# Sliding-window attention with an MLP-mixer: attention scores on half of the array's rows, the first heads loaded as float32, and new instruction orders

## The chip, the cores and the metric

The kernel runs on one core of a Trainium2 chip. The metric is the device time of one execution in microseconds (us), over several executions; the median is quoted with the lowest and highest.

## The reference, cut to what matters

```python
# B, H, S, D = 8, 8, 576, 64; window 128
scores = q @ k.T / sqrt(D) + slope[h] * -abs(i - j)     # only 0 <= i - j < 128, else -1e9
attn   = softmax(scores) @ v                            # [8, 8, 576, 64]
x  = attn, heads side by side                           # [8, 576, 512]
u  = x + (relu(x.T @ w_tok1) @ w_tok2).T                # token mix   576 -> 256 -> 576
out = u + relu(u @ w_ch1) @ w_ch2                       # channel mix 512 -> 1536 -> 512
```

A block of 128 keys meets only its own 128 queries and the next 128. That makes a 128 x 256 block of scores for each head and key block. 576 is four chunks of 128 and a tail of 64.

## The kernel before: the parts that matter

TensorE contracts over the partitions, the 128 rows of its array. A head has only D = 64 of them. The kernel keeps two heads (a "head pair") on top of each other in one `kT` tile and pads q with zeros, so that one full matmul gives both heads' scores side by side:

```python
psS = [PS(f"psS{i}", [P, 512]) for i in range(2)]      # PSUM: two score banks
psO = PS("psO", [P, 2, 512])                           # PSUM: probabilities times v
qT  = [T(f"qT{i}", [P, NC, NHP, 2, P]) for i in range(2)]   # head 0: rows 0-63, head 1: rows 64-127, rest 0
# ... cut
def score(b, kb, hp):                                  # one key block, one head pair
    # ... cut
    lhsT = kT[i][:, kb, hp, :]                         # 128 rows: head 0 over head 1
    if kb < NC - 1:
        nc.tensor.matmul(s[:, :], lhsT=lhsT, rhs=qT[i][:, kb:kb + 2, hp, :, :],   # 512 columns
                         start=True, stop=True)
    # ... cut: last key block (256 + 128 columns) and tail (128)
    nc.scalar.activation(out=e[:, 0:nn], in_=s[:, 0:nn], func=ACT.Exp, scale=scale)
    # ... cut: DVE multiplies by the mask, one head pair at a time
```

The order of all work of a batch is written out as a list of names. One prime is one batch ahead. `S` are scores, `A` transposes of q and k on TensorE (batches 0 and 1), `Lk Lq Zk Zq` loads of k and q and their DMA transposes (later batches), `v` a chunk of v, `P` probabilities times v, `K U X` the token mix, `C` and `D` the two channel matmuls, `T` and `E` their tails, `H0 H1` the two halves of the second channel weight. A list for the steady state, before:

```python
PERIOD = """
S33' T0 Zk'' C0 C1 C5 C3 P2' C7 v0''' C2 S40' Zq'' C6 P3' C4 C9 S41' C10 Lk''' v4''' C8 S42'
# ... cut
S23'' X0' S30'' E0 E1 E2 D30 D31 S31'' D32 S32''
"""
```

The softmax here doesn't subtract the row's maximum and nothing guards it: scores larger than these inputs give would overflow.

## Time and profile before

| | before |
|---|---|
| device time, median of 4 runs beside the changed kernel | 317.18 us (316.64 to 319.14) |
| profiled span | 314.4 us |
| TensorE (PE) busy, matmuls | 289.1 us, 2469 |
| first channel matmul starts | 40.08 us |
| two steady batches | 68.70 us |

How to read it: the device time is nearly all TensorE, but "busy" hides what a matmul costs. A matmul's record is about 400 ns long for 512 columns, yet the next one starts 215 ns later. So I count starts, not busy time. Two groups of the page show what the change aims at (line, engine, operation, output<-inputs, shapes, count | busy us, mean ns | idle before and what ended it):

```profile
L281 ACT ACTIVATE pe<-psS 128x512 bf16<-128x512 f32 (+2 forms) x160 | 78.2, 514 | 92.6 <-PE psS L271 37.6
L271 PE MATMUL psS<-qT,kT 128*128 128x512 bf16 x96 | 35.9, 400 | 3.4 <-ACT qT L239 1.8
```

There are 96 score matmuls that stream 512 columns each, half of them against zeros, and 160 exponentials.

### The profile page before, as it was taken

Reading aid. Unit: us, or ns where it says so; the run is one execution under the profiler, and the core shown is the slowest. Engines: PE = TensorE matmul, PEld = TensorE weight load, DVE = VectorE, ACT = ScalarE, POOL = GpSimd, SP = SyncE. Lnnn points to the kernel's source line nnn. Section 1 sums busy time; section 2 is a strip of 40 time slices with the busy share of each in tenths; the row PEclk is TensorE's granted clock in tenths of the full one; section 3 lists DMA queues with packets and bytes.
Section 4 is the critical chain, followed back from the end, with each engine's and each line's share of the span. In section 5 each row is a group of like instructions: output and inputs, shape, how many; then the busy total and the mean of one; then the engine's idle time right before and its main releaser. Section 6 shows DMA issues by size and latency. Waiting matters only on the chain.

```text
span 314.4 us, 6324 instructions
## 1 busy us (share of the span) xinstructions
PE 289.1 (92%) x2469; PEld 160.0 (51%) x2490; DVE 196.9 (63%) x478; ACT 130.5 (42%) x269; POOL 125.5 (40%) x166
## 2 busy tenths in 40 slices
PE   1677795999999999999999999999999999999995
PEld 1255543645564555546554555545554555545443
DVE  4468565958874866559674847568756937553521
ACT  4757575506442643346333552345235632212200
POOL 8996796309805950882097304850000000000000
PEclk9999999999999999999999999999999999999999
DMA  7999999989997998999499929991740120001013
GB/s 95 141 198 196 183 159 151 134 201 138 169 181 80 149 171 137 192 160 130 110 190 168 89 69 211 162 162 38 176 85 33 70 67 2 33 35 67 2 67 100
DMA packets 152381, 38.52 MB, mean 122 GB/s; under 512 B 139552, under 2 KB 147872, under 8 KB 152352
## 3 DMA queue, kind: packets, MB, share of 16 engines
q0 software_dynamic: 103664, 17.80, 82.6%
q1 hardware_dynamic: 48688, 20.32, 28.8%
q8 instruction: 19, 0.31, 0.4%
q14 instruction: 10, 0.08, 0.1%
HBM read 35.85 MB, written 9.44 MB: 144 GB/s over the span
## 4 chain that ended last, share of the span: by engine, by line
PE 78%; DMA 10%; POOL 8%; issue 2%; DVE 1%; SPq 0%; POOLq 0%
PE psM L483 25%; PE psM L435 23%; DMA vp<-in_v_dram 7%; PE psS L271 5%; PE psM L378 4%; PE psM L393 3%; PE psM L505 3%; DMA qT<-qn 3%; PE psT L450 3%; PE psO L315 2%; PE psM L425 2%; POOL vp L166 2%; PE psO L311 2%; POOL ks L176 1%; PE psM L380 1%
## 5 line engine op out<-in xcount | busy, mean ns | idle before, releaser
L281 ACT ACTIVATE pe<-psS 128x512 bf16<-128x512 f32 (+2 forms) x160 | 78.2, 514 | 92.6 <-PE psS L271 37.6
L483 PE MATMUL psM<-WC,r 128*128 128x512 bf16 x359 | 89.1, 379 | 0.7
L435 PE MATMUL psM<-utb,WC 128*128 128x512 bf16 x384 | 89.1, 379 | 0.2 <-ACT qT L239 0.2
L438 DVE TENSOR_SCALAR r<-psM 128x512 bf16<-128x512 f32 x72 | 49.6, 690 | 20.0 <-PE psM L435 18.8
L435 PEld LDWEIGHTS <-WC 128*128 128x128 bf16 x384 | 35.5, 98 | 37.4 <-issue 0.2
L483 PEld LDWEIGHTS <-r 128*128 128x128 bf16 x372 | 35.2, 98 | 37.6 <-issue 0.2
L286 DVE TENSOR_TENSOR pb<-pe,masks 128x512 bf16<-128x512 bf16 x96 | 39.4, 419 | 10.7 <-ACT pe L281 10.3
L186 POOL DMA_DIRECT2D qn<-in_q_dram x48 | 35.9, 771 | 23.2 <-DMA qT<-qn 12.8
L166 POOL DMA_DIRECT2D kn<-in_k_dram x24 | 21.1, 905 | 55.6 <-DMA kT<-kn 54.2
L488 DVE TENSOR_TENSOR ob<-psM,ub 128x512 f32<-128x512 f32 x31 | 21.4, 692 | 32.1 <-PE psM L483 31.9
L271 PE MATMUL psS<-qT,kT 128*128 128x512 bf16 x96 | 35.9, 400 | 3.4 <-ACT qT L239 1.8
L166 POOL DMA_DIRECT2D vp<-in_v_dram x32 | 29.1, 937 | 2.1 <-DMA qs<-in_q_dram 0.8
L441 ACT ACTIVATE r<-psM 128x512 bf16<-128x512 f32 x24 | 14.3, 597 | 23.1 <-PE psM L435 23.0
L395 DVE TENSOR_TENSOR ub<-psM,xb 128x512 bf16<-128x512 f32 x28 | 18.7, 684 | 2.7 <-PE psM L393 2.7
L325 DVE TENSOR_TENSOR xb<-psO,rt 128x512 bf16<-128x512 f32 x28 | 19.4, 692 | 1.0
L315 PE MATMUL psO<-vp,pb 128*128 128x65 bf16 x224 | 15.9, 193 | 3.5 <-DMA vp<-in_v_dram 3.5
L315 PEld LDWEIGHTS <-pb 128*128 128x128 bf16 x224 | 13.4, 97 | 6.8 <-issue 4.4
L393 PE MATMUL psM<-r,W 128*128 128x512 bf16 x50 | 14.4, 379 | 0.1
L378 PE MATMUL psM<-xb,W 128*128 128x512 bf16 x56 | 14.4, 379 | 0.0
L271 PEld LDWEIGHTS <-kT 128*128 128x128 bf16 x96 | 9.3, 99 | 9.8 <-issue 3.2
L450 PE MATMUL psT<-utt,WC 128*128 128x64 bf16 x384 | 13.8, 193 | 0.0
L450 PEld LDWEIGHTS <-WC 128*128 128x128 bf16 x384 | 12.9, 98 | 1.6 <-issue 0.2
(121 smaller groups left out, 338.7 us busy)
## 6 DMA issues: line engine op xcount, KB each, us to landing
out_dram<-ob SPq DMA_DIRECT2D x31, 256.0 KB, 2.2
vp<-in_v_dram POOLq DMA_DIRECT2D x32, 128.0 KB, 6.9
kn<-in_k_dram POOLq DMA_DIRECT2D x24, 128.0 KB, 6.1
qn<-in_q_dram POOLq DMA_DIRECT2D x48, 64.0 KB, 5.1
WC<-in_moe_w_ch_dram POOLq DMA_DIRECT2D x3, 512.0 KB, 9.4
WC<-in_moe_w_ch_dram POOLq DMA_DIRECT2D x2, 768.0 KB, 9.4
out_dram<-ob SPq DMA_DIRECT2D x10, 128.0 KB, 2.3
qs<-in_q_dram POOLq DMA_DIRECT2D x3, 256.0 KB, 8.1
```

The lines of the kernel that those rows point to most:

```text
L166: nc.gpsimd.dma_start(out=dst, in_=src[b, :, c * P:(c + 1) * P, :].rearrange("h s d -> s h d"))
L186: nc.gpsimd.dma_start(out=dst[:, :, 3 * i, :], in_=q[b, i::2, s0:s0 + n, :].rearrange("h s d -> s h d"))
L271: nc.tensor.matmul(s[:, :], lhsT=lhsT, rhs=qT[i][:, kb:kb + 2, hp, :, :], start=True, stop=True)
L281: nc.scalar.activation(out=e[:, 0:nn], in_=s[:, 0:nn], func=ACT.Exp, scale=scale)
L286: nc.vector.tensor_tensor(out=p[:, :], in0=e[:, :], in1=masks[:, hp].rearrange("p a i x -> p (a i x)"), op=ALU.mult)
L315: nc.tensor.matmul(ov, lhsT=probs[b, qb, hp][:, i * P:(i + 1) * P], rhs=vt[:, qb, h, :], start=first, stop=(hh == 3))
L378: nc.tensor.matmul(t[:, :], lhsT=W1[:, c, dh * P:(dh + 1) * P], rhs=xb[b % 2][:, c, :], start=(c == 0), stop=False)
L393: nc.tensor.matmul(t[:, :], lhsT=W2[:, j, c * P:(c + 1) * P], rhs=r1[b % 2][:, j, :], start=(j == 0), stop=(j == 1))
L435: nc.tensor.matmul(t[:, :], lhsT=WC1[:, cb, ht * P:(ht + 1) * P], rhs=utb[b % 2][:, :, cb, :], start=(cb == 0), stop=(cb == NCB - 1))
L438: nc.vector.tensor_scalar(out=r2[b % 2][:, ht, :], in0=t[:, :], scalar1=0.0, scalar2=None, op0=ALU.max)
L450: nc.tensor.matmul(o, lhsT=WC1[:, cb, ht * P:(ht + 1) * P], rhs=utt[(b // 2) % 2][:, cb, b % 2, :], start=(cb == 0), stop=(cb == NCB - 1))
L483: nc.tensor.matmul(t[:, :], lhsT=r2[b % 2][:, ht, c * P:(c + 1) * P], rhs=WC2[:, ht, :], start=(ht == 0), stop=(ht == NHT - 1))
```

## The change

It means to take half of the score columns away from TensorE. The two heads of a pair now use 64 rows each, in the upper and lower half of the array, and their matmuls may run at the same time. q needs no padding any more. One item is now four heads, so ACT and DVE handle 1024 elements in one instruction. The start-up is rebuilt too: q and k of the first four heads of batch 0 are loaded in float32 by SyncE and cast on chip, and the loads stand in another order.

```diff
-    psS = [PS(f"psS{i}", [P, 512]) for i in range(2)]
-    psO = PS("psO", [P, 2, 512])
+    psS = [PS(f"psS{i}", [P, 2, 512]) for i in range(2)]   # shared by scores and probabilities times v
-    qT = [T(f"qT{i}", [P, NC, NHP, 2, P]) for i in range(2)]
+    qT = [T(f"qT{i}", [P, NC + 1, NHP, P]) for i in range(2)]
@@ score @@
-                nc.tensor.matmul(s[:, :], lhsT=lhsT, rhs=qT[i][:, kb:kb + 2, hp, :, :],
-                                 start=True, stop=True)
+            for a in range(2):
+                hp = 2 * j + a
+                halves = [slice(h * D, (h + 1) * D) for h in range(2)]
+                if kb < NC - 1:
+                    for h, r in enumerate(halves):
+                        nc.tensor.matmul(s[:, h, a * 256:(a + 1) * 256], lhsT=kT[i][r, kb, hp, :],
+                                         rhs=qT[i][r, kb:kb + 2, hp, :], start=True, stop=True)
+                    continue
# ... cut: last key block and tail likewise, exponential and mask over 1024 elements
+    def load_f32(dst, src, hp):
+        hs = slice(2 * hp, 2 * hp + 2)
+        nc.sync.dma_start(out=dst[:, hs, :],
+                          in_=src[0, hs, 0:SM, :].rearrange("h (p j) d -> p h (j d)", j=4))
@@ PERIOD @@
-S33' T0 Zk'' C0 C1 C5 C3 P2' C7 v0''' C2 S40' ...
+P1' T0 Zk'' C1 C6 C9 C10 S30' S31' C0 Zq'' C4 C7 P3' C5 P2' C3 C8 v1''' T1 C11 v3''' Lk''' P4'
+C2 K0' Lq''' K1' v2''' D00 D01 D02 v4''' S01'' S00'' U0' U2' D10 v0''' D11 D12 U1' S21'' S11''
+U3' D20 X1' D21 P0'' D22 X0' UT' S20'' S10'' X2' X3' D30 D31 D32 E0 E1 E2
# ... cut: the first token matmul in halves of 256 columns with row-tiled tails, prologue and other orders
```

## The prediction

> **What bounds the kernel now.** I read three views: the page (busy shares and the 40 slices), the table of stretches cut where a batch begins its first channel matmul, and the timeline of TensorE. From the page:
>
> ```profile
> PE 289.1 (92%) x2469; PEld 160.0 (51%) x2490; DVE 196.9 (63%) x478; ACT 130.5 (42%) x269; POOL 125.5 (40%) x166
> ...
> PE   1677795999999999999999999999999999999995
> ...
> DMA  7999999989997998999499929991740120001013
> ```
>
> TensorE is full from the eighth slice (about 53 us) to the last one. Before that it has holes, and there the DMA row is full. So there are two regimes: about 53 us of start-up in which data arrives as fast as it can, then 260 us in which TensorE sets the pace. The stretches (length, then each engine's busy us) say the same:
>
> ```profile
> 0.00:20.00 20.00, 9.22 (x79) 5.20 (x80) 10.05 (x32) 11.04 (x23) 17.66 (x29) 1.00 1.26 133
> 20.00:53.00 33.00, 24.57 (x312) 15.72 (x311) 21.92 (x61) 21.27 (x46) 27.33 (x35) 1.00 1.97 176
> ...
> 152.60:188.36 35.76, 35.60 (x293) 19.41 (x294) 23.08 (x57) 14.69 (x31) 15.60 (x20) 1.00 1.29 138
> 188.36:221.31 32.95, 32.79 (x277) 17.99 (x278) 23.08 (x57) 14.10 (x30) 14.69 (x19) 1.00 1.38 137
> ```
>
> In steady state two batches take 68.71 us and TensorE idles 0.32 of them; DVE and ACT are at two thirds and under a half. Whether "busy" hides slack is told by the starts in the timeline:
>
> ```profile
> 40.08 1.89 PE L435 MATMUL psM<-utb,WC 128*128 128x512 bf16 x8 [0.19 <-ACT qT L239]
> 41.90 0.41 PE L232 MATMUL psM<-ident,ks 128*64 128x128 bf16 x8
> 42.15 0.39 PE L232 MATMUL psM<-ident,qs 128*64 128x128 bf16 x8
> 42.47 0.39 PE L271 MATMUL psS<-qT,kT 128*128 128x512 bf16 x1
> 42.70 1.89 PE L435 MATMUL psM<-utb,WC 128*128 128x512 bf16 x8
> 44.42 0.59 PE L271 MATMUL psS<-qT,kT 128*128 128x512 bf16 x2
> 44.86 0.39 PE L248 MATMUL psM<-ident,qkt 128*128 128x128 bf16 x4
> 45.08 1.03 PE L435 MATMUL psM<-utb,WC 128*128 128x512 bf16 x4
> ```
>
> From 42.70 to 44.42 eight matmuls of 512 columns take 1.72 us: one starts every 0.215 us. Four of 128 columns take 0.22 (44.86 to 45.08): 0.055 each. 256 columns lie between, 0.109; with 64 or 65 columns one starts every 0.029. I counted every matmul of the program at these four rates: 278.3 us. From 53 us to the end the real starts follow that count except for about 2 us of waits. So a column taken from TensorE after 53 us is time taken from the kernel.
>
> The start-up is told by the timeline's hole (48.41 to about 52.3) and the chain of waits:
>
> ```profile
> 26.11 10.29 DMA vp<-in_v_dram
> 36.68 1.75 POOL kn L166 x2
> ...
> 45.42 6.86 DMA vp<-in_v_dram
> 52.96 0.86 PE psM L435 x4
> ```
>
> Batch 1's v lands at 45.42 + 6.86 = 52.3 us; its first probability-times-v waits for it 3.7 us. Batch 0's first channel matmul begins at 40.08.
>
> **What the Trainium skill says.** "TensorEngine Tiling (Array Packing)", Key Properties: row or column tiles execute in parallel, but changing the tiling mode drains TensorE. The trace agrees on both, for column tiles: the transposes L232 use 64 of 128 columns, and eight of them take 0.25 us (41.90 to 42.15), 0.031 each against 0.055 untiled, so two run at once. Entering that mode costs 41.90 - (40.08 + 8 x 0.216) = 0.09; leaving costs 42.47 - (42.15 + 4 x 0.056) = 0.10; with slower first pairs I take 0.105 a switch. Same page, Gotcha 1: different row tiles must not write one PSUM bank together, which is why the new scores put the two heads into two banks. "TensorE: Matmul & The Clock Gate", Part 3: 64- or 32-row matmuls on distinct row groups run concurrently, 3.07x measured for four. No row tile runs in the kernel before, so this trace cannot confirm it. "DMA: Bandwidth & Descriptors", Queues, rings and completion order: each DMA engine goes round-robin over the queues, so loads from SyncE share the same 16 engines; I expect an earlier start from them, not more bandwidth.
>
> **The change part by part.**
>
> *Scores.* Before, q is padded with zeros: one matmul of 128 rows streams both heads' queries, 512 columns. Whole kernel: 96 x 0.216 + 32 x 0.109 + 64 x 0.056 = 27.8 us. After, each head uses its 64 rows: 192 of 256 columns, 64 of 128, 128 of 64, in pairs. With a 3 ns stagger within a pair: 96 x 0.112 + 32 x 0.059 + 64 x 0.032 = 14.7. Saved: 13.1 us.
>
> *First token matmul.* 70 x 0.216 = 15.1 becomes 112 x 0.109 plus 14 pairs x 0.112 = 13.8, because its 64-row tails are now tiled too. Saved: 1.3. Identity matmuls for one residual add and one warming matmul cost 0.4. Sum: 14.0 us less streaming.
>
> *Mode switches.* The order of TensorE's instructions has 11 changes of mode before and 90 after (about ten in a steady batch; the new orders put scores in adjacent pairs to keep this low). 79 x 0.105 = 8.3 us given back. TensorE's net gain is 14.0 - 8.3 = 5.7 us, about 0.9 in a steady batch.
>
> *Exponentials and masks.* One instruction now covers 1024 elements. ACT took 276, 498 and 600 ns for 128, 384 and 512, so I estimate 1035 for 1024: 8 x 1.035 = 8.3 us per batch against 12 x 0.600 + 4 x 0.498 + 4 x 0.276 = 10.3. The masks on DVE shrink from 7.9 to about 5.8 in the same way. Neither is on the path in steady state; it relieves start-up.
>
> *Padded q.* The zeroing memsets go (POOL 3.6 us near 18.6 to 22, 1.8 near 39; DVE 2.2 at the start), 48 loads of q become 24, and the DMA transpose of q halves. Bytes from HBM stay the same.
>
> *Start-up.* This is the larger term. Four things move: two head pairs of q and k are loaded as float32 by SyncE from 0.8 us and cast on DVE and ACT; the other four heads go next on POOL, then v; batch 2's v and the first half of the last weight now come behind batch 1's v. I add up landings with intervals seen in this trace: about 1.3 us for four heads of q or k, 1.05 for a v chunk, 2.5 to 3.5 for a third of the first channel weight, 3.2 for token weights, 0.84 for a k chunk. Batch 0's q and k are in at about 10 us (17 before), its v at 17, token weights at 20.5, batch 1's q and k at 28, all of the first channel weight at 34, batch 1's v at 42 to 43 (52.3 before: 4.6 us of batch 2's v and 3.4 of weight are behind it now, and the start is denser).
>
> Compute follows: after v at 17 to 18, DVE has about four head pairs x (1.35 normalise + 0.6 add + 0.45 copy), plus masks, some 10.5 us with its waits. So the first channel matmul starts at about 30, not 40.1.
>
> *Sum.* At the first channel matmul the count says 264.2 us of stream are left before, 259.2 after (switches in). Before: 40.1 + 264.2 + 3.7 (wait for v) + 2 (later waits) + 3.2 (last matmul to end) = 313.2, against 314.4 measured, so the count holds within 1.2. After: 30 + 259.2 + 3 (v at 42.5 for a point reached at 39.4) + 3 + 3.2 = 298.4. Timed runs are 2.9 us above the profiled span (317.36 against 314.4): 301.3. Prediction: 301 us, 5% faster.
>
> **The rivals.**
>
> *Row tiles do not overlap, or the switches eat it all.* If the 64-row pairs ran one behind another, the 13.1 us would be lost and the switches still paid: about 314, "same". Against it: column tiles overlap in this very trace. If a switch cost 0.2 instead of 0.105, another 8.5 us: about 310.
>
> *DMA stays the bound of start-up.* Total bytes are unchanged and the slices show it full to 190 us. If batch 1's v lands no earlier than 48, the end moves to about 307. For it: new waits are possible on the second weight (needed at about 49, due at 48) and on batch 2's transposes. Against it: those bytes are merely reordered behind v, and the q transposes shrink.
>
> *PSUM becomes the bound.* Scores and probability-times-v now share two slots of two banks, each score slot held for about 1.04 us of ACT, where four smaller ones were. If each steady batch lost 1 us to this, 7 us: about 308. Against it: after a pair of scores the order puts 2.6 us or more of other matmuls.
>
> *Better than thought.* If row-mode switches are nearly free, 8 us less: about 293.
>
> **Range and chances.** The start-up estimate is good to some 4 us, switches to 4, steady waits to 3; together 294 to 310. Faster by over 2% means below 311.0; it needs just one of the two gains. Faster 0.88, within 2% 0.10, slower 0.02.
>
> **What would show it.** In the new trace: scores of 256 columns starting in pairs a few ns apart, pairs about 0.11 us apart; 0.09 to 0.11 us lost on each side of a run of scores; steady pairs of batches of about 66.9 us instead of 68.7; the first channel matmul near 30 us and batch 1's v near 42; TensorE still at nine tenths afterwards. Wrong if the pairs start 0.11 us apart within themselves, if the first channel matmul stays beyond 36, or if steady batches show holes ahead of scores waiting for ACT or DVE.

## The result

The changed kernel took 300.95 us (median of 4; 299.9 to 301.49) against 317.18 for the kernel before. The ratio is 0.947 (95% interval 0.942 to 0.953). Ratios here are the mean time of one kernel's fast runs over that of the other's fast runs of the same rounds, so not quite the ratio of the medians. 301 us had been predicted.

The page of the changed kernel, the lines that answer to those of before:

```profile
PE 283.1 (95%) x2757; PEld 159.6 (54%) x2757; DVE 173.2 (58%) x341; ACT 129.0 (43%) x203; POOL 99.4 (33%) x128
...
PE   1889996999999999999999999999999999999995
...
DMA  8999999999999999984999169913501120010023
```

And the two groups that the change aims at, as they are now:

```profile
L293 ACT ACTIVATE pe<-psS 128x1024 bf16<-128x1024 f32 (+1 forms) x69 | 62.7, 966 | 37.4 <-PE psS L280 30.0
L280 PE MATMUL psS<-qT,kT 64*128 64x256 bf16 x192 | 16.5, 280 | 1.3 <-ACT pe L293 0.8
```

The holes of the start-up are nearly closed. A six remains in the seventh slice (45 to 52 us), and the list of waits below accounts for most of it; after it TensorE is at nine tenths to the last slice but one. The DMA row is as full as before. DVE and POOL have shed 24 and 26 us. In the steady batches this lay off the path. In the start-up some of it may have counted: the page gives POOL 8% of the chain that ended last before, and 1% now.

The stretches cut at each batch's first channel matmul (length, then the busy us of PE, PEld, DVE, ACT and POOL, granted clock, DMA share, GB/s):

```profile
31.75:72.20 40.45, 37.84 (x428) 21.02 (x425) 26.27 (x49) 21.66 (x33) 21.49 (x27) 1.00 1.71 164
72.20:106.74 34.54, 34.54 (x314) 18.51 (x310) 20.95 (x39) 15.29 (x22) 17.56 (x21) 1.00 1.76 157
106.74:138.79 32.05, 32.05 (x319) 17.82 (x315) 20.66 (x40) 14.38 (x21) 12.57 (x15) 1.00 1.23 129
138.79:173.65 34.86, 34.86 (x334) 19.19 (x331) 20.30 (x38) 14.95 (x22) 12.56 (x15) 1.00 1.12 124
```

From 72 us on, busy equals length: TensorE has no wait of over 0.15 us in these batches, the shortest that the profile counts. A steady pair is 32.05 + 34.86 = 66.91 us, against 68.70. Cut at the same events, the 16.2 us between the two profiled spans came from here:

| stretch | before | after | difference |
|---|---|---|---|
| start to batch 0's first channel matmul | 40.08 | 31.75 | -8.3 |
| from there to batch 2's | 79.41 | 74.99 | -4.4 |
| batch 2's to batch 7's | 167.08 | 163.03 | -4.0 |
| batch 7's to the end | 27.83 | 28.43 | +0.6 |

Half the gain is the start-up; the other half is spread over all batches. In the second row the wait for v has gone, and a new one has come. The list of waits of the kernel before has (who waited, for what: us in total, times, longest):

```profile
PE psO L315 <- DMA vp<-in_v_dram: 3.5, 1, 3.5
```

and that of the changed kernel, between 38 and 56 us:

```profile
PE psM L519 <- DMA WC<-in_moe_w_ch_dram: 2.1, 1, 2.1
```

The chain of waits shows the same (start us, length us):

```profile
36.65 14.43 DMA WC<-in_moe_w_ch_dram
51.08 0.04 issue
51.12 1.02 PE psM L519 x4
```

The second half of the second channel weight lands at 51.08, 14.4 us after its issue. TensorE had been waiting for 2 us by then.

Last, a run of scores in steady state, from the timeline of TensorE:

```profile
156.82 0.61 PE L280 MATMUL psS<-qT,kT 64*128 64x256 bf16 x8
157.36 1.04 PE L429 MATMUL psM<-r,W 128*128 128x512 bf16 x4
```

Eight 64-row matmuls of 256 columns need 0.54 us until the next matmul starts. One behind the other they would need 8 x 0.109 = 0.87. The starts, read singly from the trace, are:

```
156.816 156.820 | 156.936 156.939 | 157.045 157.048 | 157.154 157.157 | 157.359 (next, 128 rows)
```

The two matmuls of a pair start 3 to 4 ns apart, and pairs 0.109 to 0.120 us after the one before. From the start of the last pair, 0.205 us pass to the next ordinary matmul instead of 0.109: the switch out costs about 0.1.

### The profile page after: what moved, and what is told of

The parts are those of the page before. It is cut to its first block, busy times and chain, and to the rows that moved or that the text cites. A ratio compares the mean times of both kernels' runs of the same rounds, so it can differ in the third digit from the quotient of the medians.

```text
span 298.2 us, 6583 instructions
## 1 busy us (share of the span) xinstructions
PE 283.1 (95%) x2757; PEld 159.6 (54%) x2757; DVE 173.2 (58%) x341; ACT 129.0 (43%) x203; POOL 99.4 (33%) x128
## 4 chain that ended last, share of the span: by engine, by line
PE 83%; DMA 12%; POOL 1%; DVE 1%; issue 1%; SPq 0%; ACT 0%
PE psM L519 27%; PE psM L471 25%; DMA WC<-in_moe_w_ch_dram 11%; PE psM L429 4%; PE psM L404 4%; PE psS L280 4%; PE psM L541 3%; PE psT L486 3%; PE psM L461 2%; PE psS L343 2%; PE psS L339 2%; DMA qf<-in_q_dram 2%; PE psM L227 1%; PE psS L371 1%; PE psM L500 1%; PE psS L284 1%
## 5 line engine op out<-in xcount | busy, mean ns | idle before, releaser
L293 ACT ACTIVATE pe<-psS 128x1024 bf16<-128x1024 f32 (+1 forms) x69 | 62.7, 966 | 37.4 <-PE psS L280 30.0
L471 PEld LDWEIGHTS <-WC 128*128 128x128 bf16 x384 | 34.7, 98 | 37.5 <-issue 1.6
L474 DVE TENSOR_SCALAR r<-psM 128x512 bf16<-128x512 f32 x48 | 33.2, 691 | 27.5 <-PE psM L471 27.4
L299 DVE TENSOR_TENSOR pb<-pe,masks 128x1024 bf16<-128x1024 bf16 (+1 forms) x51 | 33.3, 657 | 21.0 <-ACT pe L293 20.9
L477 ACT ACTIVATE r<-psM 128x512 bf16<-128x512 f32 x48 | 27.8, 601 | 27.3 <-PE psM L471 27.2
L183 POOL DMA_DIRECT2D qn<-in_q_dram x24 | 21.2, 916 | 11.1 <-DMA qT<-qn 11.1
L464 ACT COPY utb<-psM 128x512 bf16<-128x512 bf16 x21 | 12.3, 597 | 19.8 <-PE psM L461 19.7
L489 ACT ACTIVATE r2t<-psT 128x384 bf16<-128x384 f32 x16 | 7.9, 492 | 28.7 <-PE psT L486 28.7
L353 DVE TENSOR_TENSOR xb<-psS,rt 128x512 bf16<-128x512 f32 x28 | 19.4, 692 | 1.0
L280 PE MATMUL psS<-qT,kT 64*128 64x256 bf16 x192 | 16.5, 280 | 1.3 <-ACT pe L293 0.8
L422 ACT ACTIVATE r<-psM 128x512 bf16<-128x512 f32 x7 | 4.2, 598 | 27.8 <-PE psM L413 27.8
L343 PE MATMUL psS<-vp,pb 128*128 128x65 bf16 x224 | 15.7, 193 | 0.0
```

What stands on the lines that cost most here:

```text
L183: nc.gpsimd.dma_start(out=dst, in_=src[b, :, c * P:(c + 1) * P, :].rearrange("h s d -> s h d"))
L280: nc.tensor.matmul(s[:, h, a * 256:(a + 1) * 256], lhsT=kT[i][r, kb, hp, :], rhs=qT[i][r, kb:kb + 2, hp, :], start=True, stop=True)
L293: nc.scalar.activation(out=e[:, h, :], in_=s[:, h, :], func=ACT.Exp, scale=scale)
L299: nc.vector.tensor_tensor(out=p[:, :].rearrange("p (h x) -> p h x", h=2)[:, h], in0=e[:, h, :], in1=masks[:, j, h].rearrange("p h g a x -> ...
L343: nc.tensor.matmul(ov, lhsT=prob(b, qb, h, 0), rhs=vt[:, qb, h, 0:D + 1], start=first, stop=(hh == 3))
L353: nc.vector.tensor_tensor(out=xb[b % 2][:, qb, :].rearrange("p (b h d) -> p b h d", b=2, h=4), in0=ov[:, :, :, 0:D], in1=rv[:, :, :, None] ...
```

## The experiments

All of them gave outputs that the comparison with the reference accepted. The median of the kernel before was between 317.57 and 318.35 us in their rounds. "First" is batch 0's first channel matmul, "pair" two steady batches.

| run | us, median (range) | ratio to before | first | pair |
|---|---|---|---|---|
| the change | 300.95 (299.9 to 301.49) | 0.947 | 31.75 | 66.91 |
| e1 | 301.79 (300.84 to 302.46) | 0.949 | 31.47 | 67.13 |
| e2 | 305.68 (303.4 to 306.41) | 0.961 | 31.19 | 68.60 |
| e3 | 299.18 (298.7 to 299.48) | 0.942 | 31.02 | 66.92 |
| e4 | 315.08 (313.86 to 317.24) | 0.992 | 39.34 | 68.70 |
| e5 | 311.17 (310.5 to 311.68) | 0.979 | 33.25 | 70.42 |
| e6 | 306.86 (306.53 to 307.23) | 0.966 | 40.50 | 66.91 |
| e6b | 306.40 (302.9 to 307.36) | 0.961 | 35.43 | 66.91 |
| e7 | 300.10 (299.69 to 302.43) | 0.945 | 32.56 | 66.65 |
| e8 | 300.74 (298.9 to 303.21) | 0.946 | 30.72 | 66.65 |
| e9 | 308.36 (307.77 to 308.81) | 0.969 | 31.07 | 66.91 |
| e10 | 300.99 (299.01 to 301.24) | 0.945 | 31.86 | 66.64 |
| e11 | 303.45 (301.81 to 304.54) | 0.954 | 31.14 | 67.26 |

My theory was that of the prediction: overlapping row tiles save the columns, each switch of the tiling mode gives 0.105 us back, and the new order of loads gives the start-up. Its rivals were that the overlap is not what saves, that switches cost more or less, and that waits for data come back elsewhere.

### Does the overlap save the time? (e5, e1, e11)

**e5** keeps everything but puts both heads on the upper 64 rows, so that no two score matmuls can overlap. Its scores are wrong, though the comparison with the reference did not notice.

```diff
-                halves = [slice(h * D, (h + 1) * D) for h in range(2)]
+                halves = [slice(0, D) for h in range(2)]
```

> The changed kernel with both heads of a pair read from the upper 64 rows. Wrong on purpose: odd heads get the scores of even ones. Same number of matmuls, columns and mode changes; only the second row tile is never used, so no two score matmuls can share the array. Theory (it is the overlap of the two row tiles that saves, and in the run with another order TensorE still paired them, a tile's matmul starting ahead of an earlier one that waits for its own tile): a batch streams 24 x 0.109 + 8 x 0.056 + 16 x 0.029 us instead of 12 x 0.112 + 4 x 0.059 + 8 x 0.032, 1.69 us more; steady pairs of batches 70.3 us instead of 66.9, and about 11.8 us over seven batches: 313. Rival (narrow matmuls are simply cheap, by 64 rows or by 256 columns, and the tiles need not differ): no change, within 1 us of 301.

It took 311.17 us, with steady pairs of 70.42. Its scores in the timeline:

```profile
162.95 1.04 PE L280 MATMUL psS<-qT,kT 64*128 64x256 bf16 x8
163.92 1.04 PE L429 MATMUL psM<-r,W 128*128 128x512 bf16 x4
```

The same eight matmuls now need 0.97 us instead of 0.54, and start singly, 0.109 us apart. So the overlap is worth about 10 us of the kernel. Without it a steady pair takes longer than before the change (70.42 against 68.70), and only the start-up gains. The whole came 2 us under the 313 that I expected. The theory holds to a tenth of a microsecond in the steady pair.

**e1** issues both matmuls of the upper rows first, then both of the lower rows. If matmuls started strictly in the order of issue, the second upper one would hold up the first lower one.

```diff
-            for a in range(2):
-                    for h, r in enumerate(halves):
+            for h, r in enumerate(halves):
+                for a in range(2):
```

> The changed kernel with the matmuls of a score item in another order: both of the upper 64 rows first, then both of the lower 64, instead of alternating. Same instructions, same columns, same number of mode changes, same results. Theory (the saving comes from two row tiles running at once, and matmuls start in order, so only neighbours on different rows overlap): in a group of four of 256 columns one overlap is left instead of two, and another at the seam of two adjacent items. Per batch 6 x 0.109 less 3 x 0.109 at seams, plus about 0.33 for the last key block: 0.66 us per batch, 4.6 us over the seven batches behind the start-up; about 305.5, steady pairs of batches 68.2 us instead of 66.9. Rival (the saving is only that fewer columns are streamed, whatever the order, or TensorE reorders matmuls by itself): no change, within 0.5 us of 301.

It took 301.79, not the 305.5 that I expected. Its timeline:

```profile
157.46 0.61 PE L280 MATMUL psS<-qT,kT 64*128 64x256 bf16 x8
158.00 1.04 PE L427 MATMUL psM<-r,W 128*128 128x512 bf16 x4
```

Again 0.54 us. I checked the built program: its order is upper, upper, lower, lower. Yet the starts, read singly, come in pairs 6 ns apart, one pair 0.102 to 0.119 us after the other:

```
157.455 157.461 | 157.574 157.580 | 157.683 157.690 | 157.792 157.799 | 158.000 (next, 128 rows)
```

Strictly in order, the first would have started alone. The records do not name the row tile, but e5 shows that two matmuls on the same rows start 109 ns apart. So the two of a pair lie on different rows: a matmul for the free half starts ahead of one that was issued earlier for the busy half. My premise was wrong; the order within an item costs only 0.2 us in a steady pair.

**e11** asks how far that goes: four matmuls of 128 columns on the upper rows, then four on the lower.

```diff
# ... cut: the loops over h and a change places, as in e1
+                        for u in range(2):
+                            nc.tensor.matmul(s[:, h, a * 256 + u * P:a * 256 + (u + 1) * P],
+                                             lhsT=kT[i][r, kb, hp, :],
+                                             rhs=qT[i][r, kb + u, hp, :], start=True, stop=True)
```

> Four matmuls of the upper 64 rows, then four of the lower, per score item (each of 256 columns split into two of 128). In the run with two and two, pairs still started 6 ns apart, so a matmul of the free tile passed two earlier ones of the busy tile. Theory (each row tile takes its matmuls from the queue independently, as far as the queue reaches): pairs again, steady pairs of batches near 67.1 us, about 302. Rival (only the next one or two are looked at): the first and last matmuls of a group run alone, 0.11 us or more per item is lost, steady pairs near 68.5, about 306.

The steady pair was 67.26 (67.1 expected). Starts come in pairs 13 to 20 ns apart, so by the reasoning of e1 the first lower matmul passes at least three upper ones. The whole took 303.45, 2.5 us more than the change, though the steady pair accounts for little. In the profile, 2.9 us of extra time lie between the first channel matmuls of batches 0 and 1 (43.35 against 40.45), so in the start-up. The timeline there:

```profile
51.81 1.86 PE L519 MATMUL psM<-WC,r 128*128 128x512 bf16 x4 [2.65 <-DMA WC<-in_moe_w_ch_dram]
```

The wait for the weight is 2.65 us, 0.6 longer than in the change. And the four matmuls after it, which took 1.02 us in the change, take 1.86: TensorE came out of the wait at half its rate, and its starts are back at the usual distance only at 55.1. I come back to this below.

### What does a switch cost? (e2, e7)

**e2** splits seventeen adjacent pairs of score items by putting one ordinary matmul item between them: 34 more switches of mode, no other work.

```diff
-P1' T0 Zk'' C1 C6 C9 C10 S30' S31' C0 Zq'' C4 ... S01'' S00'' U0' U2' ... S21'' S11'' U3' ... S20'' S10'' X2' X3'
+P1' T0 Zk'' C1 C6 C9 C10 S30' C0 S31' Zq'' C4 ... S01'' U0' S00'' U2' ... S21'' U3' S11'' ... S20'' X2' S10'' X3'
```

> The changed kernel with one other matmul item put between the two score items of each adjacent pair in the steady order. 34 more changes of tiling mode, the same matmuls. Theory (a change of mode costs about 0.105 us wherever it happens): 34 x 0.105 = 3.6 us, about 304.5; steady pairs of batches longer by 16 x 0.105 = 1.7 us. Rival 1 (the drain is only seen in the records and is hidden by the queue): no change. Rival 2 (a change costs more where the weights cannot be loaded ahead, 0.2 us): 6.8 us, about 308.

From batch 2's first channel matmul to batch 7's it took 166.63 us against 163.03: 3.60 us for 34 switches, 0.106 each. The steady pair is 1.69 longer, 1.7 expected. The total is 1.2 us higher than expected. The profiled run lost it ahead of batch 2: its list of waits has 2.8 us for the weight instead of 2.1, and 1.2 for a DMA transpose of keys that the change does not have.

**e7** goes the other way: it moves two score items of a steady batch to stand right behind the row-tiled tail of the first token matmul, so that they share its mode.

```diff
-C2 K0' Lq''' K1' v2''' D00 D01 D02 v4''' S01'' S00'' U0' ...
+C2 K0' Lq''' K1' S01'' S00'' v2''' D00 D01 D02 v4''' U0' ...
```

> The changed kernel with the first pair of score items in the steady order moved directly behind the row-tiled tail of the first token matmul. Two mode changes fewer in each of four batches, nothing else. Theory (a change of mode costs 0.105, and none is paid between two row-tiled items): steady pairs of batches 66.5 us instead of 66.9, 0.84 us in all, 300.1; visible in the stretches, barely in the times. Rival (the earlier scores fill the two PSUM slots or ACT at a bad moment, and TensorE waits for the relu of the token matmul): the pairs stay at 66.9 or get longer.

300.10 us, as expected, but with a steady pair of 66.65: 0.27 less instead of 0.42. The trace shows where the rest went. The scores start 0.106 us after the tail's last pair, so no switch is paid there. But at two places of a pair the `D` matmul right after `U2'` now starts 0.30 us after the matmul before it, where the change has 0.216: 0.16 us lost again. What it waits for there is not shown. The interval of its ratio (0.942 to 0.949) overlaps that of the change, so a gain is shown in the steady pair only, not in the total.

### What made the start-up shorter? (e9, e6, e6b, e4)

**e9** puts batch 2's v and one half of the second weight back ahead of batch 1's v, as they stood before, all else as in the change.

```diff
-... p0 l01' l23' p1 k0 v1' S31 k1 v3' qt' G2
-v1'' u0 u1 Lk'' v4' v2' p2 x1 v0' p3 H1 H0 Lq'' k2 x0 u2 k3 v3'' ek A0' v4''' u3
+... p0 l01' l23' p1 k0 v3'' S31 k1 v1' qt' G2
+v0'' u0 u1 H1 Lk'' v3' v2'' p2 x1 v4'' v1'' p3 v4' v2' v0' H0 Lq'' k2 x0 u2 k3 ek A0' v4''' u3
# ... cut: v4'' v0'' v2'' leave the next list, where they stood
```

> The changed kernel with one part of the start-up undone: batch 2's v and the first half of the second channel weight are loaded ahead of batch 1's v again, as in the kernel before. Theory (the order of these loads is a large part of the start-up gain): batch 1's v lands at 50 to 53 us instead of 40.6, its first use is reached at 41 and waits 8 to 10 us, while the 2.2 us wait for the weight goes; 6 to 8 us slower, 307 to 309. Rival (the DMA engines are full until 85 us, so order within the first 55 us only moves waits, as the combined reordering did): within 2 us of 301.

308.36 us, within what was expected. The list of waits:

```profile
PE psS L343 <- DMA vp<-in_v_dram: 9.6, 1, 9.6
```

v landed at 50.1 instead of 40.6. The wait for the weight vanished, because the weight now came in time. Net, the order of these loads is worth 7.4 us. Not all of it is the wait itself: TensorE ran at half its rate until 55.5, which is some 2.6 us of it (see the table of waits below).

**e6** takes the float32 loads away: the four loads go through POOL's queue with a cast to bf16 on the way, at the same places in the order.

```diff
-            for hp in range(2):
-                d[f"q{hp}"] = lambda hp=hp: load_f32(qf0, q, hp)
-                d[f"l{hp}"] = lambda hp=hp: load_f32(kf0, k, hp)
-                d[f"cq{hp}"] = ... # cut: the two casts
```

> The changed kernel with the first four heads of batch 0 loaded as bf16 by GpSimd at their places in its order, without the float32 copies and the casts. Theory (the float32 loads on another queue start the first transposes earlier and take four issues of about 0.75 us off GpSimd, but later the DMA engines are full anyway): all loads of GpSimd issue 3 us later at first, and this is partly caught up; first channel matmul 1 to 2 us later than 31.75, kernel 1 to 2 us slower, 302 to 303. Rival (the start-up is bound by bytes alone; bf16 writes half of them): same or faster by up to 1 us.

306.86 us, not the 302 to 303 that I expected. In the timeline:

```profile
17.95 0.64 PE L227 MATMUL psM<-ident,qs 128*64 128x128 bf16 x8 [7.61 <-DMA qs<-in_q_dram]
```

The load of `q1` stood behind a third of the first channel weight and two chunks of v in POOL's queue, so it landed at 17.9. That was my edit's doing in part, so it did not answer the question cleanly.

**e6b** repeats it with the four loads first in POOL's queue.

```diff
-l1 O q0 I J q23 M0 l0 l23 FC qt G0 M1 m0 ck1 v0 cq0 M2 v1 LC q1 ck0 ...
+l1 q0 l0 q1 O I J q23 M0 l23 FC qt G0 M1 m0 ck1 v0 cq0 M2 v1 LC ck0 ...
```

> As the run without float32 copies, which came out 5.9 us slower against 1 to 2 expected: there one of the four loads stood behind a weight and two chunks of v in GpSimd's queue and landed at 17.9 us. Here all four bf16 loads stand first in that queue. Theory (the float32 path is worth its separate queue: a load is not held behind the other issues of GpSimd; with the four in front, only about 3 us of GpSimd's issue time and its mask constants are in the way): the four land by about 8 us, the rest follow 1 to 2 us later than in the changed kernel, first channel matmul at 32.5 to 34, kernel 301.5 to 303.5. Rival (float32 by hardware queue and cast is faster in itself, and GpSimd's issue sets the start-up): still 305 or more.

306.40 us, with a wide range; 301.5 to 303.5 was expected, and the rival was nearer. The four loads landed early (4.6 to 7.6 us), but everything behind them came 2 to 4 us later: the token weights at 22.6 and 24.4 us instead of 19.3 and 20.8, batch 1's q and k at 33.1 instead of 28.7. The first channel matmul moved from 31.75 to 35.43. In the change the four loads leave by SyncE's queue while POOL issues the next ones; here POOL issues all of them one after the other, at 0.74 to 0.85 us each, 3.1 us in all, which fits the 2 to 4 us. A wait of 2.13 us for the second weight was still there, again followed by four matmuls of 512 columns in 1.86 us. So the float32 loads are worth 3.7 us at the first channel matmul; another 2.0 us of the profiled run lie between this and batch 1's first channel matmul, where the half rate falls. What made the other 4.6 of the 8.3 us to the first channel matmul (no padding of q, larger instructions, new orders) has no run of its own.

**e4** gives the kernel before one thing of the change, batch 1's v ahead of batch 2's.

```diff
-k0 Y' S22 A3 q01' p1 l23' q23' l01' v3'' qt'
-v1' v0'' H1 Lk'' u0 S32 N v3' v2'' v4'' v1'' v4' v0' ...
+k0 Y' S22 A3 q01' p1 l23' q23' l01' v3' qt'
+v1' v0' v4' H1 Lk'' u0 S32 N v3'' v2'' v4'' v1'' v0'' ...
```

> The kernel before with one part of the change alone: batch 1's v is loaded where batch 2's v was, ahead of the second channel weight, and batch 2's v comes later. Nothing else is moved. Theory (the order of loads is what the hole at 48.4 to 52.1 us is made of, and it is worth those 3.7 us alone; the rest of the start-up gain needs the earlier first channel matmul): v lands near 39, the hole closes, about 313.5. Rival (another wait opens right behind, the weight that lands at 55.5 or batch 2's transposes): less than 1.5 us gained, above 315.7.

315.08 us: a gain of about 2.5 us where 4 was expected. The hole at 48 us closed, but the list of waits now has

```profile
PE psS L271 <- DMA kT<-kn: 3.1, 1, 3.1
```

for batch 2's keys at 66 us. The result lies between theory and rival: the wait was partly moved, not removed. This profile is of the slowest of e4's four executions (317.24), the only one with a mean granted clock under 1.000; a half-rate stretch follows its wait. The other three took 313.86 to 315.17. Why such an order is worth 7.4 us in the changed kernel and 2.5 here was not tested.

### Can the new wait be removed? (e3, e8, e10)

**e3** loads the second weight ahead of batch 2's k, which a DMA transpose takes on at once.

```diff
-v1'' u0 u1 Lk'' v4' v2' p2 x1 v0' p3 H1 H0 Lq'' k2 ...
+v1'' u0 u1 v4' v2' p2 x1 v0' p3 H1 H0 Lk'' Lq'' k2 ...
```

> The changed kernel with the loads of batch 2's k moved behind both halves of the second channel weight. In the changed kernel the first of the second channel matmuls waits 2.2 us for that weight (it landed at 51.1), while the DMA transpose of k ran from 38 to 54 beside it. Theory (the weight is late because k's 3.8 us of loads are ahead of it and k's transpose shares its DMA engines): batch 1's v lands near 37 instead of 40.6, the weight near 44, the wait is gone, and the kernel is about 2.2 us faster, near 298.8. Rival (the bytes wait in any order, start-up is bound by the sum of the bytes): batch 2's k or q is then late for its first scores near 64 us, and the time stays within 0.5 us of 301.

299.18 us, 298.8 expected. The weight's halves landed at 40.99 and 44.79 instead of 44.99 and 51.08, and the wait is gone: batch 1's first channel matmul starts at 69.26 instead of 72.20. But the list of waits has a new line:

```profile
PE psS L280 <- DMA kT<-kn: 1.7, 1, 1.7
```

It is for batch 3's keys at 88 us. So about 3 us were gained and 1.7 given back. Of the 3 us, 0.7 lie ahead of the first channel matmul, where runs with an unchanged prologue differ by more than that. The ratio is 0.942 (0.939 to 0.944), against 0.947 (0.942 to 0.953) for the change; the two intervals just touch. It is the fastest version that I ran.

**e8** adds e7 to e3 and moves the loads of batch 3's keys ahead of two chunks of v, to remove that wait as well.

```diff
-C2 S20' C7 P0' T0 S10' C3 S30' S31' e2 C5 v2'' C0 v2''' Lk''' P1' ...
+C2 S20' C7 P0' T0 S10' C3 S30' S31' e2 C5 C0 Lk''' v2'' v2''' P1' ...
```

> The changed kernel with the second channel weight ahead of batch 2's k, batch 3's k ahead of two chunks of batch 2's and 3's v, and the scores behind the token tail. In the run with the weight ahead of k the 2.2 us wait for the weight went, but batch 3's first scores then waited 1.7 us for the transpose of its k, whose load ended at 81.5 behind chunks of v. Theory (that wait is only a matter of order among the loads): k's loads end about 2 us earlier, the wait goes, and with 0.84 us from the mode changes the kernel is near 297.3, 1.2% under the changed kernel. Rival (the DMA engines are full until 85 us, so a wait moved forward comes back somewhere else, as it did before): the time stays at 298.5 to 299.5.

300.74 us (298.9 to 303.21), 297.3 expected. The wait moved once more, now to a chunk of batch 2's v at 78 us:

```profile
PE psS L339 <- DMA vp<-in_v_dram: 4.1, 1, 4.1
```

**e10** has the edits of e3 and e7 too, but keeps batch 2's chunk in place and moves only batch 3's.

```diff
-C2 S20' C7 P0' T0 S10' C3 S30' S31' e2 C5 v2'' C0 v2''' Lk''' P1' ...
+C2 S20' C7 P0' T0 S10' C3 S30' S31' e2 C5 v2'' C0 Lk''' v2''' P1' ...
```

> The changed kernel with the second channel weight ahead of batch 2's k (alone 299.2), the scores behind the token tail (alone 300.1), and one chunk of batch 3's v behind batch 3's k. The earlier combination moved a second chunk of v as well, one that batch 2 needs at 77.6 us; it landed at 82.0 and cost a 4.1 us wait. Theory (with that chunk back in its place, only the 1.7 us wait for batch 3's k is touched, and shrinks by about 1 us; mode changes give 0.5): 298 to 298.5, about 0.9% under the changed kernel. Rival (the wait comes back elsewhere): 299 or more.

300.99 us, 298 to 298.5 expected. The keys came late again:

```profile
PE psS L280 <- DMA kT<-kn: 2.2, 1, 2.2
```

Both times the rival was right. The slices of the changed kernel show the DMA row at nine tenths from the second slice to the seventeenth, 7 to 127 us. While it is full, an order decides only who waits.

Yet e10 lost more than its wait. From batch 1's first channel matmul to batch 2's it took 38.52 us, 4.0 more than the 34.54 of the change, and the wait is 2.2 of them. Its timeline (start, length, instruction; in brackets the idle time before and what ended it):

```profile
89.72 0.61 PE L280 MATMUL psS<-qT,kT 64*128 64x256 bf16 x8 [2.23 <-DMA kT<-kn]
90.16 0.38 PE L413 MATMUL psM<-xt,W1t 64*128 64x256 bf16 x4
90.47 4.45 PE L519 MATMUL psM<-WC,r 128*128 128x512 bf16 x12
94.76 1.03 PE L429 MATMUL psM<-r,W 128*128 128x512 bf16 x4
```

and the same place in e3, where the wait was 1.68:

```profile
88.33 0.61 PE L280 MATMUL psS<-qT,kT 64*128 64x256 bf16 x8 [1.68 <-DMA kT<-kn]
88.78 0.38 PE L413 MATMUL psM<-xt,W1t 64*128 64x256 bf16 x4
89.09 2.76 PE L519 MATMUL psM<-WC,r 128*128 128x512 bf16 x11
91.69 1.03 PE L429 MATMUL psM<-r,W 128*128 128x512 bf16 x4
```

In e3 these matmuls take 91.69 - 89.09 = 2.60 us (one of the twelve has no record). In e10 twelve take 4.29 instead of 2.59: eight of them start at 0.43 us intervals, twice the usual. That is the missing 1.7 us. The page's clock row of e10, in tenths by slice, has a dip just there (the thirteenth slice, 90 to 97 us):

```profile
PEclk9999999999997999999999999999999999999999
```

I then went through all traces for waits of TensorE of over 1.5 us after 31 us, and for such stretches behind them. Each trace also records when the granted clock changed. Within one trace these moments lie whole multiples of 3.41 us apart: in e10 at 12.16, 90.67 and 94.08 us, 23 steps and 1. So here is each wait, cut by this grid of 3.41 us windows:

| run | wait, us | longest part in one window | half rate |
|---|---|---|---|
| the change | 49.07 to 51.12: 2.05 | 1.55 | none |
| e3 | 86.65 to 88.33: 1.68 | 1.68 | none |
| e7 | 49.88 to 51.56: 1.68 | 1.68 | none |
| before | 48.79 to 52.32: 3.53 | 1.78 | none |
| e2 | 49.35 to 52.12: 2.76 | 1.80 | none |
| e1 | 49.08 to 51.32: 2.24 | 1.84 | none |
| e6b | 53.11 to 55.24: 2.13 | 1.99 | 55.10 to 58.51 |
| e4 | 66.53 to 69.64: 3.12 | 2.03 | 71.02 to 74.44 |
| e10 | 87.48 to 89.72: 2.23 | 2.23 | 90.67 to 94.08 |
| e11 | 49.15 to 51.81: 2.65 | 2.44 | 51.59 to 55.00 |
| e8 | 77.99 to 82.06: 4.07 | 3.41 | 81.92 to 85.33 |
| e9 | 40.65 to 50.22: 9.57 | 3.41 | 45.26 to 55.50 |

The length of a wait does not sort these runs: 2.13 us were enough in e6b, 3.53 us were not in the kernel before. The part within one window does: half rate came from 1.99 us on, and not up to 1.84. It begins where a window ends and lasts one window (three in e9), so a window at half rate costs 1.7 us. That is a reading of twelve waits; no run moved a wait against the grid on purpose. e5 and e6 have no such wait. In the start-up less was enough: in the change, half rate from 16.49 to 23.31 us follows a window with 1.22 us of such waits.

Does this explain the range within one kernel's runs (those of e8 span 4.3 us, those of e3 0.8)? The mean granted clock of every execution is on record. The two slowest of e8 (303.21 and 302.18) have the lowest, 0.983, and its fastest (298.9) the highest, 0.994; but the fastest of e6b (302.9) has the lowest of its four, 0.989. So it explains a part at most.

## Why the prediction was right, point by point

- **The bound and the columns: right.** TensorE's starts set the time from about 53 us on. A steady pair of 66.9 us was predicted, and 66.91 came.
- **Overlap of row tiles: right.** Pairs start 3 to 4 ns apart, and e5 shows that without it about 10 us are lost.
- **Switches at 0.105 us: right.** e2 gives 0.106. The rivals "0.2 each" and "nearly free" fall. The 1.3 us of the first token matmul had no run of their own; they are right as far as the whole count is.
- **PSUM as the bound: did not come.** Steady stretches have no wait of over 0.15 us.
- **First channel matmul at about 30 us: 31.75.** This is the term that was too small by 1.75. Runs with the same prologue gave 31.1 to 32.6 (e5, with slower scores, 33.25), so part of it is spread from run to run. Whether the half rate from 16.49 to 23.31 us has a share in it is open: e10 had none there, and gave 31.86.
- **Batch 1's v at 42 to 43, a wait of 3 us: it landed at 40.6, and there was no wait,** since TensorE got there only at about 41.2, in part because the first channel matmul was late. This term was too large by 3.
- **The second weight, named as a possible wait with "needed at about 49, due at 48": it landed at 51.08, and TensorE waited 2.1 us.** It was only one of the rivals, with "3" for all later waits together; I had sized the weight's loads at the 3.4 us that each took before, and here they took 4.4 and 6.1, the second beside the transpose of batch 2's keys.
- **The sum is therefore better than its terms.** The start took 1.75 us more than predicted. For waits and for errors of the count, 298.2 - 31.75 - 259.2 - 3.2 = 4.05 us are left, where 3 + 3 had been set down; the list of waits after 31.75 us has 2.9 of them. The two errors cancel: 298.4 was computed for the span, 298.2 measured. That the sum came so close is luck.
- **The 2.9 us from span to timed runs mix two things.** The profiled execution of the kernel before took 316.28 us, 1.9 more than its span; the other 1.1 is that it was faster than the median of the timed runs. The changed kernel's profiled execution happened to be its fastest too (1.7 and 1.05 us), so the term fitted again.
- **A reading of the page that was loose:** the DMA row of the kernel before is not full "to 190 us". It has a four at 149 to 157 us and a two at 181 to 189. Nothing in the prediction hangs on it.
- **What the prediction lumped together, the experiments split.** The order of the loads with v is worth 7.4 us (e9), the float32 loads 3.7 us at the first channel matmul and 5.5 in the end (e6b). Both contain time at half rate, and they may overlap, so they are not to be added. "An earlier start, not more bandwidth" fits e6b, but when I wrote the expectations of e6 and e6b I took it for less than that, and was wrong in both.

## What to carry to other kernels

Count starts at the rate of each shape and add a fixed cost for each switch of tiling mode; in this kernel that count gave a steady stretch to a tenth of a microsecond, and it says to put the row-tiled items next to each other. While the DMA engines are full, moving a load ahead moves the wait to whatever now comes later, so look for the next reader before judging. A wait of TensorE of about two microseconds or more can cost 1.7 us beyond its length, because the clock may come back at half its rate; whether it does depended here on how the wait lay against a grid of 3.41 us, so two runs with the same wait can differ.

## What the Trainium skill lacked or had wrong

- "TensorE: Matmul & The Clock Gate", Part 3, has matmuls "pc-monotone in start AND end", that is, starting and ending in the order of the program, without reordering. Here e1 and e11 do not fit that: with upper, upper, lower, lower in the program, starts still come in pairs 6 ns apart (13 to 20 ns with four and four), and eight matmuls of 256 columns took 0.54 us as in the alternating order. The page's 4 ns from tile to tile agrees with the 3 to 4 ns of the change.
- "TensorEngine Tiling (Array Packing)", Key Properties, says that a change of mode drains TensorE, but gives no cost. Here 34 more changes took 3.60 us, 0.106 each.
- "TensorE: Matmul & The Clock Gate", Part 1, puts the throttling down to an idle window of about 3.4 us, and its section on oscillation gives the rule "no PE-idle gaps >~3.4µs". Here the half rate (0.43 us from start to start at 512 columns, 0.215 otherwise) also followed waits of 2.13, 2.23 and 2.65 us, and did not follow one of 3.53 us. The page's window that runs freely fits this, since the clock changed on a grid of 3.41 us; but it need not be idle as a whole: 1.99 us of waiting in one window were enough, 1.84 were not.
- The same Part 1 warns that clock events in a trace can be unreliable. Here none was seen to be wrong, but early ones are missing: in the kernel before, matmuls of 128 columns at 21.7 to 22.6 us start 0.107 us apart, twice the usual 0.055, while the page's clock row, `9999...`, shows no dip. Its trace has no clock record ahead of 23.23 us, where the distance falls to the usual one. The distance between starts of one shape is the safer reading.
- No page that I read says how a DMA transpose slows loads beside it. In the change the weight's second half landed 6.1 us after the first, while the transpose of batch 2's keys was under way from 38.12 to 54.06 us; in e3, ahead of that transpose, 3.8 us after. That the transpose is the reason was not tested alone.
